# A long-convolution gate: the third stage's loop over rows instead of groups, and the distance between its two halves

## The chip, the cores and the metric

One core of a Trainium2 chip. The metric is the device time of one execution in microseconds (us), the median of several runs. The engines are TensorE (PE in the profile, its weight loads PEld), VectorE (DVE), ScalarE (ACT), GpSimd (POOL) and SyncE (SP, which only issues transfers here); DMA queues hang on SP and ACT.

## The reference

Two layers, all in float32, with B = 4 sequences of S = 12800 positions and D = 128 channels. The second uses the first's output y times x as its own input:

```python
def _attn_ref(x, v, pos_emb, w1, w2):
    h_filt = (np.maximum(pos_emb @ w1, 0.0) @ w2) * np.exp(-0.01 * pos)[:, None]
    u = x * v
    y = irfft(rfft(u, 2 * S) * rfft(h_filt, 2 * S))[:, :S, :]      # causal convolution along S
    return x * y

def _moe_ref(x, w_val, conv_w, w_out):          # x: what the first layer returned
    for k in range(5):
        gate_pre += conv_w[k] * xp[:, k:k + S, :]   # 5 taps along S, per channel
    gate = 1 / (1 + exp(-gate_pre))
    return (gate * (x @ w_val)) @ w_out
```

## The kernel before, in words

The convolution is done as Fourier transforms written as matrix products over S = 2 x 100 x 64 (J x N1 x N2). The first stage forms u = x·v, transforms it along N1 and stores the spectra in DRAM (`a_u`); the second multiplies them with the filter's spectrum and stores back-transformed blocks in DRAM (`c_y`). Both are untouched. The change lies in the **third stage** (from line 530), which does the last inverse transform along N1, multiplies by x, and runs the whole second layer.

Its unit is a **row**: one n2 of 64, that is 4 x 100 = 400 values in each of 128 channels (`ROW`). Four rows make a **group** (`R = 4`); 2 x 16 groups make the output (`NT = 32`, 128 rows). Two halves run at once, one ahead of the other.

*The y half* makes a row of x·y. `y_sum` (line 592): PE multiplies the blocks of `c_y` into PSUM `sd` (two buffers); two rows' sums stand together, at every second row. `y_copy` (601): ACT copies `sd` to `sd_sb`. Two rows later (`LAG = 2`) `y_trans` (606): PE transposes into `tp`, ACT copies a part to `dif`. `y_join` (615): DVE makes `yr` in two instructions (620, 621), POOL multiplies with x into `ext` (623). `ext` holds a block of 16 rows behind 4 rows of halo. The halo is filled by ACT (`fill_halo`, 576) once in four groups, after the last row of the block's first group is under way: one copy of 1600 wide (line 588), four narrower ones for the first block of a half (583 to 586), and one more copy of 1600 for the last (590). In each half of 16 groups the last group comes first, into a tile of its own, `tail`, because the first block's halo needs it.

*The gate half* reads 4 groups' rows from `ext`. `tap(t, 0)` (635): ACT starts group t's gate `gt` with the first tap, 1600 wide. `tap(t, 1)` to `tap(t, 4)` (638): DVE adds one tap to the whole group, one in each row's turn; tap k needs the group's first k rows. `sigmoid` (642): ACT, 1600 wide, after tap 4. In the next group's turn, row by row: `value` (647) PE into `v_ps`, `gated` (652) DVE into `gd`, one row later `project` (657) PE into `o_ps`, one more row later `finish` (665) ACT copies into `o_sb`, and after the fourth row ACT issues the group's store (668).

The order is written out by hand (`tc.manual_schedule()`): each engine executes its instructions in the order in which the loop records them, and waits only for semaphores. The loop (684) goes over groups, with four rows inside; the y half works on group `s = t + AHEAD3`, three groups, that is 12 rows, ahead of the group t that gets its taps. So the row r of a y group is always recorded together with the row r of a gate group: the sums stand with r = 0 and 2, the first tap of the next group and the sigmoid with r = 3, and the halo copy with r = 3 too, behind the sigmoid. Loads of the next blocks of `c_y` and of x (`load_rows`) are issued by SP, which waits there for free buffers.

Of the kernel before, what the change touches and what calls it, by code (L numbers as in the profile page):

```python
# [9 lines left out]
F32 = mybir.dt.float32  # L10
# [18 lines left out]
R = 4  # L29
# [92 lines left out]
def tile_longconv_gate(  # L122
# [407 lines left out]
    with tc.tile_pool(name="p3", bufs=1) as p3, tc.tile_pool(name="ps3", bufs=1, space=PSUM) as ps3:  # L530
# [17 lines left out]
        def load_rows(s):  # L548
            j, g = y_order[s]
            ct = []  # L550
            for c in range(2):
                t = block(s, c)
                ct.append(t)
                if s < FIRST:
                    continue
                n0 = c * N2 + g * R
                rows_ = c_y[j].rearrange("k p b d -> k p (b d)")
                for h in range(0, R, R // 2):
                    sync_s.dma_start(
                        out=t[:, h * B * D:(h + R // 2) * B * D],  # L560
                        in_=rows_[:, n0 + h:n0 + h + R // 2].rearrange("k p e -> k (p e)"))
            if s not in loads3:
                load_x(s)
            loads3[s] = ct, loads3[s]
# [27 lines left out]
        def y_sum(s, r):  # L592
            ct, _ = loads3[s]
            sd = ps3.tile([128, B * D], F32, name="sd", bufs=2)
            for c in range(2):
                nc.tensor.matmul(  # L596
                    out=sd[c * N2:(c + 1) * N2], lhsT=inv[:, c], rhs=ct[c][:, r * B * D:(r + 1) * B * D],
                    start=True, stop=True)
            sds[s, r] = sd

        def y_copy(s, r):
            t = p3.tile([128, B, D], F32, name="sd_sb", bufs=3)
            nc.scalar.copy(out=t.rearrange("p b d -> p (b d)"), in_=sds.pop((s, r)))  # L603
            sds[s, r] = t

        def y_trans(s, r):
            t = sds.pop((s, r))
            tp = ps3.tile([D, B, 128], F32, name="tp3", bufs=2)
            for b in range(B):
                nc.tensor.transpose(out=tp[:, b], in_=t[:, b], identity=ident)  # L610
            dif = p3.tile([D, B, NC1], F32, name="dif", bufs=3)
            nc.scalar.copy(out=dif, in_=tp[:, :, N2:N2 + NC1])
            tps[s, r] = tp, dif
# [17 lines left out]
        def tap(t, k):  # L631
            if k == 0:
                gt = p3.tile([D, R * ROW], F32, name="gt", bufs=2)
                gate_gt[t] = gt
                nc.scalar.activation(gt, rows(t, 0), AF.Copy, scale=cw[:, 0:1])  # L635
            else:
                gt = gate_gt[t]
                nc.vector.scalar_tensor_tensor(gt, rows(t, k), cw[:, k:k + 1], gt, op0=ALU.mult, op1=ALU.add)  # L638

        def sigmoid(t):  # L640
            sg = p3.tile([D, R * ROW], F32, name="sg", bufs=2)
            nc.scalar.activation(sg, gate_gt.pop(t), AF.Sigmoid)  # L642
            gate_sg[t] = sg

        def value(t, r):
            v_ps = ps3.tile([D, ROW], F32, name="v_ps", bufs=2)
            nc.tensor.matmul(out=v_ps, lhsT=wval, rhs=rows(t)[:, r * ROW:(r + 1) * ROW], start=True, stop=True)  # L647
            return v_ps

        def gated(t, r, v_ps):  # L650
            gd = p3.tile([D, ROW], F32, name="gd", bufs=2)
            nc.vector.tensor_tensor(gd, v_ps, gate_sg[t][:, r * ROW:(r + 1) * ROW], op=ALU.mult)  # L652
            return gd

        def project(gd):
            o_ps = ps3.tile([D, ROW], F32, name="o_ps", bufs=2)
            nc.tensor.matmul(out=o_ps, lhsT=wout, rhs=gd, start=True, stop=True)  # L657
            return o_ps

        def finish(t, r, o_ps):  # L660
            if r == 0:
                o_sb = p3.tile([D, R * ROW], F32, name="o_sb", bufs=2)
                outs3[t] = o_sb
            o_sb = outs3[t]
            nc.scalar.copy(out=o_sb[:, r * ROW:(r + 1) * ROW], in_=o_ps)  # L665
            if r == R - 1:
                j, g = groups[t]
                nc.scalar.dma_start(
                    out=out[j][:, g * R:(g + 1) * R].rearrange("d n b a -> d (n b a)"), in_=outs3.pop(t))

        AHEAD3, NT, LAG = 3, len(groups), 2
        y_run, gd_last, o_last = [], None, None
        with tc.manual_schedule():
            for s in range(2):
                load_x(s)
            load_rows(0)

            for _ in range(WARM):  # L680
                w_ps = ps3.tile([D, 2 * D], F32, name="o_ps", bufs=2)
                nc.tensor.matmul(
                    out=w_ps, lhsT=ident, rhs=dft.rearrange("p a k -> p (a k)"), start=True, stop=True)
            for t in range(-AHEAD3, NT + 2):
                s = t + AHEAD3
                if s + 1 < NT:
                    load_rows(s + 1)
                if 0 <= s < NT:
                    j, g = y_order[s]
                    if g == NG - 1:  # L690
                        tails[j] = p3.tile([D, R, B, N1], F32, name="tail", bufs=2)
                    elif g % EG == 0:
                        new_ext(j, g // EG)
                for r in range(R):
                    done = y_run.pop(0) if len(y_run) == LAG or s >= NT and y_run else None
                    if done:
                        y_trans(*done)
                    v_ps = value(t - 1, r) if 0 <= t - 1 < NT else None
                    if o_last is not None:
                        finish(*o_last)  # L700
                        o_last = None
                    if gd_last is not None:
                        o_last = gd_last[0], gd_last[1], project(gd_last[2])
                        gd_last = None
                    if s < NT and r % 2 == 0:
                        y_sum(s, r)
                        y_sum(s, r + 1)
                    if 0 <= t < NT:
                        tap(t, r + 1)
                    if r == R - 1 and 0 <= t + 1 < NT:  # L710
                        tap(t + 1, 0)
                    if v_ps is not None:
                        gd_last = t - 1, r, gated(t - 1, r, v_ps)
                    if done:
                        y_join(*done)
                    if s < NT:
                        y_copy(s, r)
                        y_run.append((s, r))
                    if r == R - 1 and 0 <= t < NT:
                        sigmoid(t)  # L720
                    if r == R - 1 and s < NT and g % EG == 0:
                        fill_halo(j, g // EG)


_INS = ["w1", "w2", "moe_w_val", "moe_conv_w", "moe_w_out"]
# [44 lines left out]
```

## Time and profile before

| what | value |
|---|---|
| median of three runs | 1163.94 us (1157.94, 1163.94, 1168.69) |
| profiled execution | 1167.67 us, its span 1165.5 us |
| third stage | from about 766 us to the end |
| busy in the span | PE 1046.1, DVE 969.3, POOL 775.2, ACT 615.7 us |
| busy, 900 to 1000 us | PE 97.0, DVE 96.3, POOL 88.8, ACT 72.5 of 100 us; DMA 0.94 |

The span goes from the first to the last instruction; the execution's own time is 2.2 us longer. In a row of the timeline the first number is the start in us, the second the duration; several instructions of one kind that follow each other are merged (x2). "idle before" in brackets is the time for which the engine had nothing to run, with what ended it. A duration includes the engine's pipeline, so that the next instruction can start up to 0.1 us before it ends; how often an engine can start an instruction is read from start to start.

### The profile page before, as it was taken

What the parts mean: (1) busy time and instruction counts of PE and PEld (TensorE: products, weight loads), DVE (VectorE), ACT (ScalarE), POOL (GpSimd) and SP (SyncE); (2) the same over time, 40 slices, a digit from 0 to 9 for tenths busy, and PEclk for the clock granted to TensorE, in tenths of its full rate; (3) what the DMA queues carried; (4) which work ended last, traced back from release to release, by engine and by line L of the source; (5) the groups of instructions that cost most, each with busy time, mean ns of one, the idle gap of its engine ahead of it and who ended that gap; (6) DMA issues with size and microseconds to landing.
All of it is one profiled execution on the core that took longest, in us unless ns stands there. A gap on an engine that the chain in (4) does not pass through costs nothing.

```text
span 1165.5 us, 17562 instructions
## 1 busy us (share of the span) xinstructions
PE 1046.1 (90%) x6208; PEld 492.1 (42%) x6208; DVE 969.3 (83%) x1150; ACT 615.7 (53%) x1000; POOL 775.2 (67%) x393
## 2 busy tenths in 40 slices
PE   4899887887764999999999999979999999999986
PEld 2455543443321444444444444434444444444432
DVE  5675445798944899999999999629999999999996
ACT  1366555665641344444444444346676767677763
POOL 3354332323313888889888889737889898898880
PEclk9999999998995899999999999988999999999999
DMA  9999999999987588988888998558999999999932
GB/s 364 350 417 403 361 352 345 353 341 350 344 268 286 209 311 300 317 300 302 303 312 287 362 339 321 178 176 218 283 288 285 264 292 278 278 289 284 284 119 113
DMA packets 92888, 344.60 MB, mean 296 GB/s; under 512 B 9774, under 2 KB 19418, under 8 KB 77610
## 3 DMA queue, kind: packets, MB, share of 16 engines
q1 hardware_dynamic: 58824, 263.74, 69.1%
q10 hardware_dynamic: 33978, 79.74, 17.8%
q8 instruction: 51, 0.84, 0.3%
q14 instruction: 35, 0.29, 0.1%
HBM read 212.37 MB, written 131.07 MB: 295 GB/s over the span
## 4 chain that ended last, share of the span: by engine, by line
PE 58%; DMA 28%; ACT 6%; DVE 4%; issue 2%; SPq 1%; ACTq 0%; DVEq 0%
PE c_ps L435 21%; DMA a_u<-st 19%; PE sd L596 9%; PE z_ps L419 9%; DMA ld<-in_xv_dram 6%; PE o_ps L657 6%; PE v_ps L647 5%; PE tp L610 5%; PE c_ps L404 2%; DVE gt L638 2%; PE fp L334 2%; ACT gt L635 1%; ACT o_sb L665 1%; DMA c_y<-c_sb 1%; ACT sg L642 1%
## 5 line engine op out<-in xcount | busy, mean ns | idle before, releaser
L623 POOL TENSOR_TENSOR ext<-yr,xr 128x400 f32<-128x400 f32 x120 | 301.6, 2515 | 44.0 <-DVE yr L621 41.9
L322 POOL TENSOR_TENSOR eo<-eo 128x512 f32<-128x512 f32 x62 | 116.8, 1904 | 212.0 <-DVE eo L321 212.0
L334 PE MATMUL fp<-eo,fold 64*128 64x512 f32 x768 | 194.4, 640 | 54.5 <-ACT st L336 40.1
L638 DVE SCALAR_TENSOR_TENSOR gt<-ext,cw,gt 128x1600 f32<-128x1600 f32 x128 | 241.5, 1887 | 0.8 <-ACT gt L635 0.8
L442 ACT COPY c_sb<-c_ps 128x1024 f32<-128x1024 f32 x100 | 101.3, 1013 | 204.6 <-PE c_ps L435 196.5
L336 ACT COPY st<-fp 128x1024 f32<-128x1024 f32 x128 | 124.2, 1015 | 133.2 <-DMA a_u<-st 81.5
L435 PE MATMUL c_ps<-va,ld 64*128 64x512 f32 (+1 forms) x800 | 166.6, 556 | 0.1
L425 DVE TENSOR_TENSOR va<-z_ps,h_sb 128x2048 f32<-128x2048 f32 x50 | 114.3, 2286 | 38.7 <-DMA ld<-a_u 30.4
L504 POOL TENSOR_TENSOR va<-va,vb 128x1024 f32<-128x1024 f32 x50 | 118.4, 2367 | 40.0 <-DVE vb L425 40.0
L419 PE MATMUL z_ps<-ld 64*64 64x512 f32 x800 | 122.4, 621 | 18.2 <-DMA ld<-a_u 16.3
L334 PEld LDWEIGHTS fp<-eo,fold 64*128 64x128 f32 x768 | 74.8, 197 | 135.8 <-issue 76.4
L596 PE MATMUL sd<-ag,inv 100*64 100x512 f32 x512 | 128.7, 620 | 1.6 <-ACT sd_sb L603 1.0
L657 PE MATMUL o_ps<-gd,wout 128*128 128x400 f32 x256 | 112.4, 521 | 19.7 <-DVE gd L652 10.9
L435 PEld LDWEIGHTS c_ps<-va,ld 64*128 64x128 f32 x800 | 74.2, 189 | 113.7 <-issue 110.2
L506 POOL TENSOR_TENSOR va<-va,vb 128x1024 f32<-128x1024 f32 x50 | 118.3, 2367 | 0.0
L603 ACT COPY sd_sb<-sd 128x512 f32<-128x512 f32 x128 | 76.1, 595 | 76.8 <-PE sd L596 54.1
L425 DVE TENSOR_TENSOR vb<-z_ps,h_sb 128x2048 f32<-128x2048 f32 x50 | 114.0, 2280 | 0.0
L647 PE MATMUL v_ps<-ext,wval 128*128 128x400 f32 x256 | 107.1, 500 | 0.0
L435 PE MATMUL c_ps<-vc,ld 64*128 64x512 f32 x400 | 94.2, 589 | 0.0
L610 PEld LDWEIGHTS tp<-ident,sd_sb 128*128 128x128 f32 x512 | 60.1, 144 | 78.9 <-PE sd L596 47.9
L505 POOL TENSOR_TENSOR vc<-vc,vd 128x768 f32<-128x768 f32 x50 | 91.2, 1824 | 2.2 <-issue 0.3
L610 PE MATMUL tp<-ident,sd_sb 128*128 128x128 f32 x512 | 81.9, 286 | 5.4 <-ACT sd_sb L603 3.8
(84 smaller groups left out, 1452.1 us busy)
## 6 DMA issues: line engine op xcount, KB each, us to landing
ld<-in_xv_dram SPq DMA_DIRECT2D x64, 1024.0 KB
c_y<-c_sb ACTq DMA_DIRECT2D x100, 512.0 KB
ld<-a_u SPq DMA_DIRECT2D x49, 1024.0 KB
a_u<-st SPq DMA_DIRECT2D x64, 768.0 KB
ag<-c_y SPq DMA_DIRECT2D x116, 384.0 KB
out_dram<-o_sb ACTq DMA_DIRECT2D x32, 800.0 KB
xr<-in_xt_dram SPq DMA_DIRECT2D x31, 800.0 KB
ld<-in_tab_w_dram SPq DMA_DIRECT2D x12, 768.0 KB
```

Source lines behind the costliest of these rows:

```text
L334: nc.tensor.matmul(out=fp[:, h], lhsT=fold[r, w], rhs=eo[r, o, :, l], start=i == 0, stop=i == len(terms) - 1)
L336: nc.scalar.copy(out=st[:, o].rearrange("k j (h b) d -> k h j (b d)", h=2), in_=fp)
L419: nc.tensor.matmul(out=zs[c][half[h]], lhsT=wk[half[c], 0, half[h]], rhs=a2[half[c], h, j], start=True, stop=True)
L425: nc.vector.tensor_tensor(out, z.rearrange("p (b d) -> p b d", d=D).unsqueeze(1).to_broadcast([128, n, B, D]), h_sb.unsqueeze(2).to_broadc ...
L435: nc.tensor.matmul(out=c_ps[:, h, 0:n], lhsT=wk[half[h], 1 + c], rhs=vt[half[h]].rearrange("p b d -> p (b d)"), start=(i == 0), stop=(i == ...
L504: nc.gpsimd.tensor_tensor(va[:, 0:2], va[:, 0:2], vb[:, 0:2], op=ALU.add)
L596: nc.tensor.matmul(out=sd[c * N2:(c + 1) * N2], lhsT=inv[:, c], rhs=ct[c][:, r * B * D:(r + 1) * B * D], start=True, stop=True)
L610: nc.tensor.transpose(out=tp[:, b], in_=t[:, b], identity=ident)
L623: nc.gpsimd.tensor_tensor(e[:, r0 + r], yr, xr, op=ALU.mult)
L638: nc.vector.scalar_tensor_tensor(gt, rows(t, k), cw[:, k:k + 1], gt, op0=ALU.mult, op1=ALU.add)
L647: nc.tensor.matmul(out=v_ps, lhsT=wval, rhs=rows(t)[:, r * ROW:(r + 1) * ROW], start=True, stop=True)
L657: nc.tensor.matmul(out=o_ps, lhsT=wout, rhs=gd, start=True, stop=True)
```

## The change

The loop goes over single rows. The y half's place (s, r) and the gate half's (t, rt) are both worked out from the row's number i, the second from i - 9: `AHEAD3` is 9 and counts rows. What is recorded within a row, and its order, is the same. Since 9 = 2·4 + 1, row r of a y group now stands together with row rt = r - 1 of a gate group: the first tap and the sigmoid (rt = 3) with r = 0, the halo copy (r = 3) with rt = 2, one row ahead of the next group's first tap and not behind the sigmoid. For the last group the sigmoid is four instructions of 400, and its output goes in three stores: rows 0 and 1, row 2, row 3.

```diff
         def sigmoid(t):
-            sg = p3.tile([D, R * ROW], F32, name="sg", bufs=2)
-            nc.scalar.activation(sg, gate_gt.pop(t), AF.Sigmoid)
+            sg, gt = p3.tile([D, R * ROW], F32, name="sg", bufs=2), gate_gt.pop(t)
+            step = ROW if t == NT - 1 else R * ROW
+            for c in range(0, R * ROW, step):
+                nc.scalar.activation(sg[:, c:c + step], gt[:, c:c + step], AF.Sigmoid)
             gate_sg[t] = sg
...
-            if r == R - 1:
-                j, g = groups[t]
+            j, g = groups[t]
+            r0 = {NT - 1: {1: 0, 2: 2, 3: 3}}.get(t, {R - 1: 0}).get(r)
+            if r0 is not None:
                 nc.scalar.dma_start(
-                    out=out[j][:, g * R:(g + 1) * R].rearrange("d n b a -> d (n b a)"), in_=outs3.pop(t))
+                    out=out[j][:, g * R + r0:g * R + r + 1].rearrange("d n b a -> d (n b a)"),
+                    in_=o_sb[:, r0 * ROW:(r + 1) * ROW])
...
-        AHEAD3, NT, LAG = 3, len(groups), 2
+        AHEAD3, NT, LAG = 9, len(groups), 2
...
-            for t in range(-AHEAD3, NT + 2):
-                s = t + AHEAD3
-                if s + 1 < NT:
-                    load_rows(s + 1)
-                if 0 <= s < NT:
+            for i in range(R * NT + AHEAD3 + R + 3):
+                (s, r), (t, rt) = divmod(i, R), divmod(i - AHEAD3, R)
+                if r == 0 and s < NT:
+                    if s + 1 < NT:
+                        load_rows(s + 1)
...
-                for r in range(R):
-                    done = y_run.pop(0) if len(y_run) == LAG or s >= NT and y_run else None
...
-                    if 0 <= t < NT:
-                        tap(t, r + 1)
-                    if r == R - 1 and 0 <= t + 1 < NT:
-                        tap(t + 1, 0)
...
+                if 0 <= t < NT:
+                    tap(t, rt + 1)
+                if rt == R - 1 and 0 <= t + 1 < NT:
+                    tap(t + 1, 0)
...
+                if s < NT:
+                    y_copy(s, r)
+                    y_run.append((s, r))
+                if rt == R - 1 and 0 <= t < NT:
+                    sigmoid(t)
+                if r == R - 1 and s < NT and g % EG == 0:
+                    fill_halo(j, g // EG)
```

Behind the diff line 642 becomes 644, 647 becomes 649, 652 becomes 654, 657 becomes 659, 665 becomes 667 and 668 becomes 671.

The order on ACT, at the start of the stage, before: from the last copy of the first halo (`tail`) to the first sigmoid's table.

```order
L586 COPY ext<-tail 128x16
L612 COPY dif<-tp_5574 128x204
L603 COPY sd_sb<-sd 128x512
L612 COPY dif<-tp_5593 128x204
L603 COPY sd_sb<-sd 128x512
L612 COPY dif<-tp_5606 128x204
L603 COPY sd_sb<-sd 128x512
L612 COPY dif<-tp_5625 128x204
L635 ACTIVATE gt<-ext,cw 128x1600
```

The same place in the changed kernel:

```order
L586 COPY ext<-tail 128x16
L612 COPY dif<-tp_5574 128x204
L635 ACTIVATE gt<-ext,cw 128x1600
L603 COPY sd_sb<-sd 128x512
L612 COPY dif<-tp_5595 128x204
```

The first tap (635) stood behind four `dif` copies after the halo; now it stands behind one.

The order on ACT where the second block of the first half gets its halo (line 588), before, with the numbers of the buffers:

```order
L612 COPY dif_5922<-tp3_5917 128x204
L665 COPY o_sb_5898<-o_ps_5900 128x400
L635 ACTIVATE gt_5930<-ext_5495,cw_73 128x1600
L603 COPY sd_sb_5938<-sd_5905 128x512
L642 ACTIVATE sg_5940<-gt_5817 128x1600
L588 COPY ext_5839<-ext_5495 128x1600
L612 COPY dif_5958<-tp3_5953 128x204
```

The same place in the changed kernel:

```order
L603 COPY sd_sb_5966<-sd_5934 128x512
L588 COPY ext_5865<-ext_5495 128x1600
L612 COPY dif_5984<-tp3_5979 128x204
L667 COPY o_sb_5955<-o_ps_5957 128x400
L635 ACTIVATE gt_5998<-ext_5865,cw_73 128x1600
L603 COPY sd_sb_6006<-sd_5991 128x512
L644 ACTIVATE sg_6008<-gt_5885 128x1600
L612 COPY dif_6015<-tp3_6010 128x204
```

Before, the three wide instructions (635, 642, 588) stand in one row, ahead of the next row's `dif`. Now the halo copy ends the row before, and the next row's `dif` and `o_sb` copies stand between it and the other two.

The end of ACT's order, before, from the last group's sigmoid on:

```order
L642 ACTIVATE sg<-gt 128x1600
L665 COPY o_sb<-o_ps 128x400 x2
L668 DMA out_dram<-o_sb 128x1600
L665 COPY o_sb<-o_ps 128x400 x4
L668 DMA out_dram<-o_sb 128x1600
```

And in the changed kernel:

```order
L644 ACTIVATE sg<-gt 128x400 x4
L667 COPY o_sb<-o_ps 128x400 x2
L671 DMA out_dram<-o_sb 128x1600
L667 COPY o_sb<-o_ps 128x400 x2
L671 DMA out_dram<-o_sb 128x800
L667 COPY o_sb<-o_ps 128x400
L671 DMA out_dram<-o_sb 128x400
L667 COPY o_sb<-o_ps 128x400
L671 DMA out_dram<-o_sb 128x400
```

The four parts of the sigmoid all stand ahead of the two copies of the group before; the last two rows get a store each.

More of the change, by code (lines that the diff above doesn't have):

```diff
@@ L693, in tile_longconv_gate @@
                         new_ext(j, g // EG)
-                for r in range(R):
-                    done = y_run.pop(0) if len(y_run) == LAG or s >= NT and y_run else None
[L696 to L707, printed above, removed]
-                    if 0 <= t < NT:
-                        tap(t, r + 1)
-                    if r == R - 1 and 0 <= t + 1 < NT:
-                        tap(t + 1, 0)
[L712 to L722, printed above, removed]
@@ new lines, in tile_longconv_gate @@
+                done = y_run.pop(0) if len(y_run) == LAG or s >= NT and y_run else None
+                if done:
+                    y_trans(*done)
+                v_ps = value(t - 1, rt) if 0 <= t - 1 < NT else None
+                if o_last is not None:
+                    finish(*o_last)
+                    o_last = None
+                if gd_last is not None:
+                    o_last = gd_last[0], gd_last[1], project(gd_last[2])
+                    gd_last = None
+                if s < NT and r % 2 == 0:
+                    y_sum(s, r)
+                    y_sum(s, r + 1)
@@ new lines, in tile_longconv_gate @@
+                if 0 <= t < NT:
+                    tap(t, rt + 1)
+                if rt == R - 1 and 0 <= t + 1 < NT:
+                    tap(t + 1, 0)
+                if v_ps is not None:
+                    gd_last = t - 1, rt, gated(t - 1, rt, v_ps)
+                if done:
+                    y_join(*done)
+                if s < NT:
[3 more added lines that the diff above has]
+                    sigmoid(t)
```

## The prediction

> **What bounds the kernel now.** I read busy time by stretch first, then the third stage's timeline, then the waits and the chain that ended last. The first two stages are untouched, so only the time from 766 us on counts. Two regular pairs of rows:
>
> ```profile
> 844.57:850.21 5.64, 5.64 (x26) 2.62 (x25) 5.64 (x10) 4.43 (x10) 5.23 (x3) 1.00 1.03 287
> 850.21:855.86 5.65, 5.65 (x26) 2.63 (x25) 5.65 (x10) 3.36 (x7) 5.23 (x3) 1.00 0.95 296
> ```
>
> The columns are the stretch, its length, busy PE, PEld, DVE, ACT and POOL, the granted clock, the DMA share and GB/s. In a regular pair PE and DVE are both full. The timeline of VectorE over one row shows which of the two sets the pace:
>
> ```profile
> 842.00 1.87 DVE L638 SCALAR_TENSOR_TENSOR gt<-ext,cw,gt 128x1600 f32<-128x1600 f32 x1
> 843.79 0.56 DVE L652 TENSOR_TENSOR gd<-v_ps,sg 128x400 f32<-128x400 f32 x1
> 844.27 0.36 DVE L620 TENSOR_TENSOR yr<-tp,dif 128x204 f32<-128x204 f32 x1
> 844.55 0.35 DVE L621 TENSOR_TENSOR yr<-tp,dif 128x196 f32<-128x196 f32 x1
> 844.82 1.87 DVE L638 SCALAR_TENSOR_TENSOR gt<-ext,cw,gt 128x1600 f32<-128x1600 f32 x1
> ```
>
> From start to start: tap 1.79, gated product 0.48, the two `yr` 0.28 and 0.27; the row is their sum, 2.82 us, with no gap. VectorE is the bound; PE fills the same time but waits for `gd` in it. So the question for every part is where VectorE, from its first tap to its last, stands still. In the steady part that is one place:
>
> ```profile
> DVE yr L620 <- ACT dif L612: 10.1, 7, 2.4
> ...
> 819.32 1.53 ACT gt L635
> ...
> 959.47 1.53 ACT gt L635
> ...
> 1006.03 1.53 ACT gt L635
> ...
> 1123.61 1.53 ACT gt L635
> ```
>
> Seven waits of 10.1 us in all, the only ones of VectorE between 801 and 1131 us. The first and the last of the chain rows are 26 groups apart: 304.29 us, where 104 rows of 2.8215 (two rows took 5.643) make 293.4. The excess, **10.9 us**, is these seven waits and what little follows them; they are the seven halo copies after the first.
>
> **Why a halo stops VectorE, and what the new phase does to it.** ScalarE's row with a first tap (before: r = 3) and, for one with a halo, the end of that row:
>
> ```profile
> 842.25 0.33 ACT L612 COPY dif<-tp 128x204 f32<-128x204 f32 x1 [0.82 <-PE tp L610]
> 842.48 0.50 ACT L665 COPY o_sb<-o_ps 128x400 f32<-128x400 f32 x1
> 842.86 1.64 ACT L635 ACTIVATE gt<-ext,cw 128x1600 f32<-128x1600 f32 x1
> 844.40 0.58 ACT L603 COPY sd_sb<-sd 128x512 f32<-128x512 f32 x1
> 844.86 1.55 ACT L642 ACTIVATE sg<-gt 128x1600 f32<-128x1600 f32 x1
> 846.30 0.34 ACT L612 COPY dif<-tp 128x204 f32<-128x204 f32 x1
> ...
> 868.88 1.53 ACT L588 COPY ext<-ext 128x1600 f32<-128x1600 f32 x1
> 870.30 0.35 ACT L612 COPY dif<-tp 128x204 f32<-128x204 f32 x1
> ...
> 870.75 0.37 DVE L620 TENSOR_TENSOR yr<-tp,dif 128x204 f32<-128x204 f32 x1 [0.99 <-ACT dif L612]
> ...
> 1105.14 0.37 DVE L620 TENSOR_TENSOR yr<-tp,dif 128x204 f32<-128x204 f32 x1 [2.42 <-ACT dif L612]
> ```
>
> From start to start: `dif` 0.23, `o_sb` 0.38, tap 1.54, `sd_sb` 0.46, sigmoid 1.44, halo 1.42. Without a halo the next `dif` starts at 846.30 and is ready at 846.64, and its `yr` would run at 847.10: 0.46 spare. A halo adds 1.42, so VectorE waits 0.96 (0.99 in the row); two copies add 2.84, so 2.38 (2.42). The account closes, so I use it for the new order.
>
> Zero is now the start of VectorE's tap in the heavy row, which is r = 0. Before, it stands at 842.00, and PE's `tp` lets the heavy row's `dif` start at 0.25; two sums stand ahead of that `tp`. In the new order no sums stand ahead of r = 0's `tp`, but they do ahead of the row before, so that row (zero at -2.82) has `dif` from -2.57, `o_sb` -2.34 and `sd_sb` -1.96 to -1.50. Without a halo the heavy row then runs with nothing late. With one:
>
> halo -1.50, `dif` -0.08, `o_sb` 0.15, tap 0.53, `sd_sb` 2.07, sigmoid 2.53 to 4.08, next `dif` 3.97 to 4.31.
>
> VectorE needs the heavy row's `dif` at 2.27, the sigmoid at 2.82 + 1.79 = 4.61 and the next `dif` at 5.09. All are there; the tightest has 0.53 spare. The halo is hidden in ScalarE's idle time ahead of the heavy row. Two copies push by another 1.42: the sigmoid ends at 5.50, VectorE waits **0.89**, twice. The four narrow copies of the second half's first block take 0.3 more than one (959.47 to 1006.03, 46.56 for 16 rows with this halo; with a single copy 45.14 + 1.1): within the spare. So of 10.9 us 1.8 stay: **-9.1**. Bounds: -10.9 if the double copies are hidden too, 0 if the wait only changes its name. I take the middle of the account, since it gave both old waits to 0.04.
>
> **The shorter lead itself.** Taps wait for products of POOL. A row's product ends a row after its join (POOL, 5.23 busy in the pair's 5.64, runs one to a row); tap k follows the join of its last row by 3 rows now, by 6 before. Two rows of cover are left; the price if they went is one shift of the pipeline, not one in each row. The start and the drain change:
>
> ```profile
> 780.02 0.34 ACT L612 COPY dif<-tp 128x204 f32<-128x204 f32 x1
> 780.24 0.60 ACT L603 COPY sd_sb<-sd 128x512 f32<-128x512 f32 x1
> ...
> 784.63 1.63 ACT L635 ACTIVATE gt<-ext,cw 128x1600 f32<-128x1600 f32 x1
> ...
> 786.30 2.32 DVE L638 SCALAR_TENSOR_TENSOR gt<-ext,cw,gt 128x1600 f32<-128x1600 f32 x1 [0.47 <-ACT gt L635]
> ...
> 1140.51 1.87 DVE L638 SCALAR_TENSOR_TENSOR gt<-ext,cw,gt 128x1600 f32<-128x1600 f32 x1
> 1142.30 0.56 DVE L652 TENSOR_TENSOR gd<-v_ps,sg 128x400 f32<-128x400 f32 x1
> 1142.79 1.87 DVE L638 SCALAR_TENSOR_TENSOR gt<-ext,cw,gt 128x1600 f32<-128x1600 f32 x1
> ```
>
> The first tap now stands right behind the `dif` of 780.02, so it starts at 780.24, where `sd_sb` did, and not at 784.63: 4.4 earlier, and VectorE's first tap with it. Three rows of the y half that ran ahead of the taps now run beside them: each costs VectorE two `yr`, 0.55, together 1.6 (a drain row is 2.28, a full one 2.82). **-2.8**. Bounds: -4.4 if the `yr` find gaps, 0 if what `sd_sb` loses behind the early tap holds up the next rows.
>
> **The end.** The last sigmoid, what waits for it, and the last store:
>
> ```profile
> 1153.80 1.54 ACT L642 ACTIVATE sg<-gt 128x1600 f32<-128x1600 f32 x1 [2.52 <-DVE gt L638]
> 1155.24 0.87 ACT L665 COPY o_sb<-o_ps 128x400 f32<-128x400 f32 x2
> 1155.36 1.22 DVE L652 TENSOR_TENSOR gd<-v_ps,sg 128x400 f32<-128x400 f32 x2 [1.12 <-ACT sg L642]
> ...
> 1156.08 0.91 PE L657 MATMUL o_ps<-gd,wout 128*128 128x400 f32 x2
> ...
> 1161.23 0.34 ACTq L668 DMA_DIRECT2D out_dram<-o_sb  x1
> ...
> 1162.00:1163.00 1.00, 0.00 (x0) 0.00 (x0) 0.00 (x0) 0.00 (x0) 0.00 (x0) 1.00 0.97 410
> 1163.50:1164.00 0.50, 0.00 (x0) 0.00 (x0) 0.00 (x0) 0.00 (x0) 0.00 (x0) 1.00 1.03 410
> ```
>
> The parts give `gd` its first row about 1 us sooner. But project 1156.08 also needs the `o_ps` buffer that the first of the two copies frees, and these copies stand behind all four parts, which at the 0.38 of a 400-wide copy take 1.52, not 1.44. It gains what the copy lets through: about **-0.1** (bounds +0.3 and -1). The store: issued 1161.23, data from 1162 to 1164, the span's end 1165.5. A quarter of the bytes takes 0.5 of the 2.0: **-1.5**, if the two stores ahead, issued about 2.3 and 1 us earlier, are through; were the three in series, each with the 0.8 ahead and the 1.5 behind its data, it would be 1158.9 + 3.3 + 2.8 + 2.8 = 1167.8, +2.3. I take -1.5, since data ran at 410 GB/s as soon as it came. The Trainium skill has a rule against the split: "DMA: Bandwidth & Descriptors", "Rules for kernel authors", tells to join many small transfers, since under 64 KB they are mostly overhead; its "Anatomy of one DMA" gives a fixed part of about 2.0 us for each. The trace's own fixed part is 0.8 + 1.5 = 2.3, for one store; whether three overlap no row here shows, and a row's store has 200 KB. By the page's 2.0, an estimate with the fixed parts in series, the end would be 1158.9 + 3.0 + 2.5 + 2.5 = 1166.9, +1.4 and not -1.5.
>
> **The sum.** -9.1 - 2.8 - 0.1 - 1.5 = -13.5. On the profiled execution: 1167.67 - 13.5 = 1154.2. It stands 3.7 above the median of 1163.94; from the median, **1150.5 us**, 1.2% faster.
>
> **The rivals.** *A. The halo's time stays.* The wait goes to another place, or to the transfers: the DMA shares above, 1.03 and 0.95 in two regular pairs, are near full, and four groups with the wait in them may be what the transfers can do. Against it: no wait of PE for a load of `c_y` stands in the steady part, and three groups of four already run without the halo's pause. Then -4.4: 1159.5.
>
> *B. The clock.* At the stage's start PE runs at half clock for 6.8 us:
>
> ```profile
> 785.90:789.30 3.40, 1.67 (x8) 0.63 (x9) 3.00 (x4) 2.32 (x6) 1.08 (x2) 0.93 1.01 310
> 789.30:792.70 3.40, 3.38 (x10) 1.47 (x12) 3.40 (x4) 0.65 (x3) 3.40 (x2) 0.50 1.03 242
> 792.70:796.10 3.40, 3.40 (x14) 1.95 (x10) 3.40 (x5) 1.28 (x3) 3.40 (x2) 0.56 0.38 72
> ```
>
> A stretch with PE busy 1.67 of 3.40 precedes it, and it costs nothing, since VectorE stays full: these rows have no `value` and `project` yet. The earlier tap holds PE up earlier. If the slow stretch falls on full rows, where PE's work fills the row at full clock, half its 6.8 us is lost: +3.4, 1153.9. The Trainium skill, "TensorE: Matmul & The Clock Gate", Part 1, says that an idle window of some 3.4 us halves the clock; here a half-idle one came before it.
>
> *C. Slower.* The sigmoid now stands between the copies of the two sums, (s, 0) and (s, 1). PE's next sums (r = 2, 0.52 behind that row's tap, so at 6.16) need both buffers. By the account with a halo, (s, 1) is copied from 4.58 to 5.2, one us ahead. If ScalarE is over 1 us later than that, PE waits in each group. Such waits in the stage now:
>
> ```profile
> PEld sd L596 <- ACT sd_sb L603: 3.8, 5, 1.9
> ```
>
> That is 0.76 each; 31 groups make 23.6, which swallows the halo's gain: 1163.9 - 4.4 + 23.6 = 1183.1. Against it: without a halo the sigmoid starts as tap 4 ends, at 1.9, 0.6 sooner, so three groups in four have over 1.5 us to spare.
>
> **How the numbers follow.** Forecast 0.66, A 0.18, B 0.10, C 0.06. A measurement of this kernel can tell about 1% from no change; 1% is 11.6 us, at 1152.3. Two thirds of the forecast's cases and a third of B's lie below that: 0.47, with a little for fills and ends that do better, 0.49. C is slower: 0.06. The rest, 0.45, is within 1%. The range: the bounds add to -10.9 - 4.4 - 1.0 - 1.5 = -17.8 (1146.1), and A lies at 1159.5; with a us more on either side for the spread of the median, 1145 to 1160.5. C is left out.
>
> **What would show it.** Right: VectorE's waits for `dif` gone but for two of about 0.9, now for the sigmoid; the heavy rows' chain rows 45.15 apart; the first tap 14.3 behind the first `tp`, not 18.7; the last store's issue to the end under 3 us. Wrong: waits of PE for `sd_sb` or for loads in each group, or a half clock behind the first `project`.

## The result and the profile after

| what | before | after |
|---|---|---|
| median of four runs each | 1164.89 us (1157.94 to 1168.69) | **1148.27 us** (1147.54 to 1149.53) |
| ratio, with its 95% interval | | **0.9859** (0.9825 to 0.9893) |
| profiled execution | 1167.67 us | 1147.54 us |
| first `tp` of the third stage, on PE | 765.97 us | 760.08 us |
| from there to the end of the execution's span | 399.5 us | 385.7 us |

Faster by 1.4%; 1150.5 was forecast. Ratios, here and below, leave out executions in which the chip ran in a slower state. The profiled executions differ by 20.1 us, but only **13.8** of them lie in the third stage, the only part that the change touches. 5.9 us went before its first `tp`, in stages whose code is the same (0.4 lie outside the two spans): in 14 traces of this study that `tp` starts anywhere between 755.3 and 766.0 us, with no regard to the kernel. So everything below is measured from the stage's first `tp` or first `yr` (1.5 us later), and not from the total.

The steady part of the stage first: busy PE, PEld, DVE, ACT and POOL between 800 and 1100 us, then the granted clock, the DMA share and GB/s. Before:

```profile
800.00:1100.00 300.00, 292.57 (x1232) 134.31 (x1232) 291.96 (x414) 210.93 (x372) 268.12 (x103) 1.00 0.94 279
```

After:

```profile
800.00:1100.00 300.00, 298.36 (x1270) 138.17 (x1269) 298.43 (x425) 218.13 (x381) 271.76 (x106) 1.00 0.97 289
```

VectorE stood still for 8.0 us of these 300 before and stands still for 1.6 now; the number of its instructions in brackets shows that it got 11 more of them through. The waits of VectorE of the changed kernel between 796 and 1112 us are one line, where before there were seven waits for `dif`, of 10.1 us:

```profile
DVE gt L638 <- ACT gt L635: 1.6, 2, 0.8
```

Two waits are left, as forecast, but for ScalarE's first tap and not for its sigmoid. They belong to the two double halo copies. Here is the first, on ACT and DVE (start, duration, engine and line):

```profile
907.27 1.55 ACT L588 COPY ext<-ext 128x1600 f32<-128x1600 f32 x1
...
908.70 1.54 ACT L590 COPY ext<-tail 128x1600 f32<-128x1600 f32 x1
...
910.12 0.35 ACT L612 COPY dif<-tp 128x204 f32<-128x204 f32 x1
910.34 0.52 ACT L667 COPY o_sb<-o_ps 128x400 f32<-128x400 f32 x1
910.53 0.57 DVE L654 TENSOR_TENSOR gd<-v_ps,sg 128x400 f32<-128x400 f32 x1
910.73 1.67 ACT L635 ACTIVATE gt<-ext,cw 128x1600 f32<-128x1600 f32 x1
...
912.43 2.01 DVE L638 SCALAR_TENSOR_TENSOR gt<-ext,cw,gt 128x1600 f32<-128x1600 f32 x1 [0.79 <-ACT gt L635]
```

The two copies, the next `dif` and `o_sb` come in the order that the prediction's list gave, and the first tap is done at 912.40, just ahead of the VectorE tap that needs it. A single halo is hidden altogether. These two first taps of ScalarE have one between them:

```profile
852.11 1.64 ACT L635 ACTIVATE gt<-ext,cw 128x1600 f32<-128x1600 f32 x1
...
897.28 1.64 ACT L635 ACTIVATE gt<-ext,cw 128x1600 f32<-128x1600 f32 x1
```

45.17 us for four groups, and the forecast was 45.15.

The stage's start, in the profiled execution:

```profile
760.08 1.11 PE L610 MATMUL tp<-ident,sd_sb 128*128 128x128 f32 x4 [3.81 <-ACT sd_sb L603]
...
775.27 0.34 ACT L612 COPY dif<-tp 128x204 f32<-128x204 f32 x1
775.49 1.65 ACT L635 ACTIVATE gt<-ext,cw 128x1600 f32<-128x1600 f32 x1
...
777.17 1.97 DVE L638 SCALAR_TENSOR_TENSOR gt<-ext,cw,gt 128x1600 f32<-128x1600 f32 x1 [0.82 <-ACT gt L635]
```

The first tap stands right behind the one `dif`, 15.4 us after the first `tp`, where 14.3 was forecast and 18.7 was the old distance. In a second trace of the same kernel (below, as a repeat) it is 14.1. The 1.3 us between the two is the granted clock. Here are the second pair of sums and the two microseconds from 6 us behind the first `tp` on (the clock is the third number from the end), first in this trace:

```profile
766.63 2.75 PE L596 MATMUL sd<-ag,inv 100*64 100x512 f32 x8
...
766.08:768.08 2.00, 2.00 (x7) 0.76 (x8) 1.27 (x4) 0.95 (x3) 1.11 (x2) 0.50 1.04 244
```

And in the repeat:

```profile
771.45 1.94 PE L596 MATMUL sd<-ag,inv 100*64 100x512 f32 x8
...
771.41:773.41 2.00, 2.00 (x11) 0.57 (x10) 1.28 (x4) 1.35 (x4) 1.21 (x2) 1.00 1.04 256
```

The stage starts at half clock in every trace, and the first transposes and sums are slow by it. Here the half clock lasted until 8.2 us behind the first `tp`, in the repeat until 5.5, so that one more pair of sums fell into it (2.75 us and not 1.94), and part of the transposes ahead of it (1.97 and not 1.45).

And the end, from the last sigmoid on:

```profile
1135.53 1.81 ACT L644 ACTIVATE sg<-gt 128x400 f32<-128x400 f32 x4 [2.52 <-DVE gt L638]
1137.24 0.86 ACT L667 COPY o_sb<-o_ps 128x400 f32<-128x400 f32 x2
...
1143.01 0.34 ACTq L671 DMA_DIRECT2D out_dram<-o_sb  x1
```

The span ends at 1145.8, 2.8 us behind the issue of the last store and not 4.3.

### The profile page after: what moved, and what is told of

Same layout as the page of the kernel before. It is cut to its first block, busy times and chain, and to the rows that moved or that the text cites. A ratio compares the mean times of both kernels' runs of the same rounds, so it can differ in the third digit from the quotient of the medians.

```text
span 1145.8 us, 17528 instructions
## 1 busy us (share of the span) xinstructions
PE 1041.9 (91%) x6208; PEld 490.5 (43%) x6208; DVE 969.1 (85%) x1150; ACT 615.9 (54%) x1003; POOL 781.2 (68%) x393
## 4 chain that ended last, share of the span: by engine, by line
PE 66%; DMA 24%; DVE 5%; ACT 3%; issue 1%; SPq 0%; ACTq 0%; DVEq 0%
PE c_ps L435 22%; DMA a_u<-st 13%; PE sd L596 10%; PE z_ps L419 9%; DMA ld<-in_xv_dram 8%; PE o_ps L659 7%; PE v_ps L649 6%; PE tp L610 5%; PE fp L334 3%; PE c_ps L404 2%; DMA ld<-in_pos_dram 2%; DVE gt L638 1%; DVE fk L284 1%; ACT st L336 1%; PE gp L292 1%
## 5 line engine op out<-in xcount | busy, mean ns | idle before, releaser
L322 POOL TENSOR_TENSOR eo<-eo 128x512 f32<-128x512 f32 x62 | 120.0, 1954 | 204.6 <-DVE eo L321 204.6
L659 PE MATMUL o_ps<-gd,wout 128*128 128x400 f32 x256 | 111.5, 517 | 10.7 <-DVE gd L654 8.7
```

Of the source, the lines that this page charges most:

```text
L322: eng.tensor_tensor(eo[:, s, :, 0], eo[:, s, :, 0], eo[:, s, :, 1], op=ALU.subtract)
```

## The experiments

Every kernel has the third stage's start and end in its trace, so beside the device times this table gives, for each, stretches in us: from the first `yr` to VectorE's first tap; from there to the tap that follows the first gated product (the first group's inside); on to the last tap; from the last tap to the end of the span; and the sum, which is called the stage below. The expectations of ctl12, halo_r0_12, lead13 and lead9 count the stage from the first `tp`, 1.5 us earlier.

| kernel | to first tap | first group | to last tap | end | sum |
|---|---|---|---|---|---|
| before | 18.82 | 15.10 | 350.49 | 13.61 | 398.02 |
| after | 15.58 | 13.00 | 343.45 | 12.18 | 384.21 |
| ctl12: lead 12 | 18.92 | 15.10 | 350.50 | 13.62 | 398.14 |
| halo_r0_12: lead 12, halo moved | 17.95 | 15.10 | 341.38 | 13.63 | 388.06 |
| lead13 | 19.69 | 13.89 | 341.25 | 13.64 | 388.47 |
| lead11 | 16.58 | 13.08 | 347.30 | 13.63 | 390.59 |
| lead11_store2 | 16.59 | 13.07 | 342.52 | 13.63 | 385.81 |
| lead9 | 15.63 | 13.01 | 343.44 | 13.63 | 385.71 |
| lead9_store0 | 14.16 | 13.00 | 377.15 | 13.69 | 418.00 |
| lead8 | 13.38 | 14.68 | 352.56 | 13.67 | 394.29 |
| end12: lead 12, new end | 19.12 | 15.09 | 350.52 | 12.12 | 396.85 |
| lead9_store: lead 9, stores split | 14.65 | 13.45 | 343.45 | 12.08 | 383.63 |
| after, again | 14.25 | 13.00 | 343.43 | 12.10 | 382.78 |
| best | 14.37 | 13.00 | 341.42 | 11.73 | 380.52 |

The first column differs by up to 1.5 us between executions with the same order. That is the clock again: of the six with 9 rows, after and lead9 had the half clock until 8.2 and 8.5 us behind the first `tp` and show 15.6, the other four until 5.2 to 6.2 us, with 14.2 to 14.7. The other columns repeat to 0.1 where nothing but that start differs (lead9_store's first group excepted).

**The loop alone** (ctl12): the loop over rows with the old distance and the old end.

```diff
-        AHEAD3, NT, LAG = 9, len(groups), 2
+        AHEAD3, NT, LAG = 12, len(groups), 2
...
-            step = ROW if t == NT - 1 else R * ROW
+            step = R * ROW
...
-            r0 = {NT - 1: {1: 0, 2: 2, 3: 3}}.get(t, {R - 1: 0}).get(r)
+            r0 = {R - 1: 0}.get(r)
```

> The row loop with the y half 12 rows ahead and the end as before: every engine's order is that of the kernel before, only line numbers differ. Theory: no change, ratio 1.000 +- 0.003, third stage (first transpose to the span's end) 399.5 us. Rival (part of the change's 16.6 us lies in the first two stages, because the program was built anew): 0.997, with the first transpose about 3 us or more earlier than 766 us.

1163.78 us beside 1163.15, ratio 1.0011 (0.9987 to 1.0035), and every stretch of the stage within 0.1 us of before. Its waits of VectorE:

```profile
DVE yr L620 <- ACT dif L612: 10.1, 7, 2.4
DVE gd L654 <- ACT sg L644: 0.7, 1, 0.7
DVE gt L638 <- ACT gt L635: 0.4, 1, 0.4
```

So writing the loop over rows does nothing; all the rest comes from the distance and the end.

**The halo copy alone** (halo_r0_12): still 12 rows ahead, but each halo copy is recorded one row later, so that it no longer stands behind the first tap and the sigmoid in the same row.

```diff
-                if r == R - 1 and s < NT and g % EG == 0:
-                    fill_halo(j, g // EG)
+                sh = (i - R) // R
+                if r == 0 and 0 <= sh < NT and y_order[sh][1] % EG == 0:
+                    fill_halo(y_order[sh][0], y_order[sh][1] // EG)
```

> Lead of 12 rows and end as before; only the halo copy stands one row later, at the end of row r = 0 and not behind the sigmoid of r = 3. Theory (ScalarE's three wide copies in one row stop VectorE): single halos cost nothing, the two double ones about 0.7 us each; third stage 399.5 - 9.5 = 390 us, ratio 0.992. Rival (the gain is the shorter lead's own): no gain, ratio 1.000. Rival (transfers set the pace of the steady part): no gain either, and waits of PE for loads of c_y appear.

1155.81 us, ratio 0.9938 (0.9915 to 0.9961). The stretch to the last tap falls by 9.1 us and the waits for `dif` from seven to two:

```profile
DVE yr L620 <- ACT dif L612: 1.4, 2, 0.7
```

One copy's place in ScalarE's order is worth what the prediction gave to the halos, with the lead and all else unchanged. VectorE has no wait that it did not have before. ScalarE's waits that the profile puts down to loads of `c_y` rise from 5.9 to 16.6 us, but they don't reach VectorE. From the first `tp` the stage is 389.6 us; 390 was expected.

**The phase without a shorter lead** (lead13): 13 rows have the same phase as 9 (r of the y half stands with rt = r - 1), but are longer than 12.

```diff
-        AHEAD3, NT, LAG = 9, len(groups), 2
+        AHEAD3, NT, LAG = 13, len(groups), 2
```

with the old end.

> Lead of 13 rows: the same phase of the two halves as with 9 (13 = 3*4 + 1), but a lead that is longer than before. End as before. Theory: the halo's part of the gain stays (-8.7 us), one more row of lead costs 0.9 us (1.45 of a row ahead of the taps, less 0.55 for two yr): third stage 391.7 us, ratio 0.993. Rival (the lead itself makes the gain, about 4 us a row): slower than before, 403.5 us, ratio 1.003.

Six runs from 1138.93 to 1165.99 us, ratio 0.986 (0.979 to 0.993): too wide for much. The trace says more: 388.5 where ctl12, the same loop, has 398.1. So 9.7 of the gain come with a **longer** lead, and the phase carries them. From the first `tp` it is 390.0, 1.7 better than expected.

**The change without its end** (lead9).

```diff
-        AHEAD3, NT, LAG = 13, len(groups), 2
+        AHEAD3, NT, LAG = 9, len(groups), 2
```

against lead13, with the old end.

> The change without its end: lead of 9 rows, the last group's sigmoid and store whole. Theory: the end is worth 1.4 us, so third stage 385.7 + 1.4 = 387.1 us, 15.2 us behind 9 would be the kernel before with the first stages' difference; ratio 0.9875 where the whole change has 0.9859. From the last tap's start to the span's end 13.6 us as before. Rival (the end is worth nothing, its three receipts come one after another): 385.7 us and the same ratio as the whole change.

1151.62 us, ratio 0.9907 (0.9874 to 0.9941); stage 385.7, or 387.2 from the first `tp`, where 387.1 was expected. Against lead13, four rows at equal phase are 2.8 us. But this trace is one of the two with the longer half clock at its start, and lead13 is not; the repeat of the change with the old end's 1.5 us put back would have 384.3, and four rows then are 4.2 us. So a row of lead is worth **0.7 to 1.0 us**, the three rows of the change 2.1 to 3.1, and the rest of the gain over ctl12, 10.3 to 10.7, goes with the phase (with what happens inside the first group, below).

**One row less** (lead8): the phase in which r of both halves is the same, as before, with the halo copy taken to the end of r = 2, ahead of the heavy row.

```diff
-        AHEAD3, NT, LAG = 9, len(groups), 2
+        AHEAD3, NT, LAG = 8, len(groups), 2
...
-                if r == R - 1 and s < NT and g % EG == 0:
+                if r == 2 and s < NT and g % EG == 0:
```

> Lead of 8 rows, so that row r of a y group stands with row r of a gate group again (8 = 2*4), as with 12; the halo copy is recorded at the end of row r = 2, the last place ahead of the tap that reads it. End as before. Theory (the phase decides, not the lead): the halo copy must wait for POOL's product of the row before it, 2.82 us behind that row's tap, the first tap then ends at 3.67 where VectorE's next group wants it at 2.82: a wait of about 0.85 us at each of seven halos, and up to 0.1 us in rows where taps now meet POOL's products; third stage from the first yr to the span's end 385.7 (lead 9) - 0.7 + 6 = 391 us or more, slower than lead 9 although the lead is shorter. Rival (every row of lead less gains): 385 us.

1161.07 us in one execution, stage 394.3: 8.6 over lead9, although it starts its taps earlier. The waits of VectorE, and the one of ScalarE that causes them:

```profile
DVE gt L638 <- ACT gt L635: 6.3, 6, 1.4
DVE yr L620 <- ACT dif L612: 1.7, 2, 0.8
DVE gt L638 <- POOL ext L623: 1.2, 1, 1.2
```

```profile
ACT ext L588 <- POOL ext L623: 3.1, 6, 0.5
```

The halo copies, one row earlier in the y group, now wait for POOL to finish the last row that they copy, and the first tap stands behind them; nine waits of VectorE, 9.2 us where lead9 has 1.6, make up most of the 8.6. Here the shorter lead does not pay, because its phase leaves the halo no free place.

**Two rows more** (lead11): another phase, r with rt = r + 1.

```diff
-        AHEAD3, NT, LAG = 9, len(groups), 2
+        AHEAD3, NT, LAG = 11, len(groups), 2
```

with the old end.

> Lead of 11 rows: the first tap and the sigmoid stand with r = 2, the halo copy with r = 3, one row behind them and not in their row. End as before. Theory: any phase but r = rt keeps the halo from VectorE; between lead 13 (388.5 us from the first yr to the span's end) and lead 9 (385.7), so 387.1 us, with waits for dif gone in the steady part. Rival (only the phase of 9 and 13 does it): about 397 us, with seven waits for dif of 10 us in all.

1153.0 us in one execution; stage 390.6, and 387.1 was expected: a miss. VectorE waits for 6.1 us between 796 and 1112 us where lead9 has 1.6. The trace shows ScalarE standing still, in waits that the profile puts down to whatever came last; none of these three is in lead9:

```profile
ACT sd_sb L603 <- DMA ag<-c_y: 40.8, 11, 5.7
ACT sd_sb L603 <- PE tp L610: 28.9, 10, 3.4
ACT sd_sb L603 <- PE v_ps L649: 17.0, 5, 4.0
```

One of them with SyncE's issues beside it (SPq and ACTq rows are issues of transfers):

```profile
821.75 5.50 SPq L118 DMA_DIRECT2D ag<-c_y  x8
...
823.83 0.50 ACT L667 COPY o_sb<-o_ps 128x400 f32<-128x400 f32 x1
...
828.47 0.34 ACTq L671 DMA_DIRECT2D out_dram<-o_sb  x1
...
828.85 0.58 ACT L603 COPY sd_sb<-sd 128x512 f32<-128x512 f32 x1 [4.53 <-DMA ag<-c_y]
```

`o_sb` is complete at 824.33, and the group's store that is to follow is issued at 828.47, after SyncE's eight loads of the next block. ScalarE executes in order, so `sd_sb` stood behind it for 4.5 us. The 32 stores of lead11 are issued 2.9 us in the median, and at most 5.3, behind the end of the `o_sb` copy ahead of them; in lead9 it is 0.03 us, and never more than 0.04. With 11 rows the store is recorded with r = 0, where SyncE issues the next group's loads; with 9 it is recorded with r = 2. That was a theory after the fact, so the last two kernels move nothing but the store.

**The store out of the loads' way, and into it** (lead11_store2, lead9_store0): each group's store is recorded two rows later, and the last one at its old place.

```diff
+                if late and late[0][0] <= i:
+                    _, dst, src = late.pop(0)
+                    nc.scalar.dma_start(out=dst.rearrange("d n b a -> d (n b a)"), in_=src)
...
             if r0 is not None:
-                nc.scalar.dma_start(
-                    out=out[j][:, g * R + r0:g * R + r + 1].rearrange("d n b a -> d (n b a)"),
-                    in_=o_sb[:, r0 * ROW:(r + 1) * ROW])
+                late.append((i + (2 if t < NT - 1 else 0), out[j][:, g * R:(g + 1) * R], o_sb))
```

> The lead of 11 rows, the end as before, and each group's store recorded two rows later, with r = 2 and not with r = 0 of the y half; the last group's store stays at its end. Theory: at a lead of 11 the stage was 3.5 us longer than its place on the line between 13 and 9 rows, because ScalarE stood behind the store's issue while SyncE issued the next group's eight loads. Two rows later these loads are out: ScalarE's waits put down to the loads of c_y (40.8 us, 11 times) go, and from the first yr to the end 390.6 becomes 387.1 (386.5 to 388). Rival: the time goes with the row in which the heavy work stands (first tap and sigmoid with r = 2, behind the sums of r = 0) and not with the store: 390.6, and the waits stay under another name.

> The lead of 9 rows, the end as before, and each group's store recorded two rows later, with r = 0 and not with r = 2 of the y half, just ahead of the first tap of the heavy row. Theory: r = 0 is where SyncE issues the next group's loads, so the store's issue holds ScalarE up there, by up to 4 us in a group and in the row with the least spare: from the first yr to the end 385.7 becomes at least 395 (up to 425), with waits of VectorE for ScalarE's first tap. Rival: the place of the store does not matter, 385.7 within 1 us; then what cost time at 11 rows was the place of the heavy row.

Both go with the theory. lead11_store2: 1150.86 us, stage 385.8 (387.1 was the middle of the expectation, 386.5 its lower end), 4.8 less than lead11, and ScalarE's waits put down to loads are gone. It is that short although a slower clock cost this execution 2.0 us early on (under the rivals, below). Between 800 and 1100 us VectorE has not one gap:

```profile
800.00:1100.00 300.00, 300.00 (x1280) 140.92 (x1279) 300.00 (x428) 223.87 (x387) 276.26 (x106) 1.00 0.96 287
```

lead9_store0: 1176.56 us, stage 418.0, **32.3 us longer** than lead9 for the same instructions with the store two rows later; at least 395 was expected. ScalarE waits in nearly every group ahead of the first tap, and VectorE behind it:

```profile
ACT gt L635 <- DMA xr<-in_xt_dram: 50.4, 23, 3.3
```

```profile
823.61 6.09 SPq L118 DMA_DIRECT2D ag<-c_y  x8
...
827.94 0.34 ACTq L705 DMA_DIRECT2D out_dram<-o_sb  x1
...
828.33 1.63 ACT L635 ACTIVATE gt<-ext,cw 128x1600 f32<-128x1600 f32 x1 [2.33 <-DMA xr<-in_xt_dram]
...
829.99 1.88 DVE L638 SCALAR_TENSOR_TENSOR gt<-ext,cw,gt 128x1600 f32<-128x1600 f32 x1 [1.07 <-ACT gt L635]
```

25 such waits of VectorE make 29.5 us. The store was issued here while the last of SyncE's eight loads was still to come (it starts at 829.46), so it does not simply queue behind all of them; what the two queues share, no trace here shows.

**The new end alone** (end12): lead 12, with the sigmoid and the stores of the last group in parts.

```diff
-        AHEAD3, NT, LAG = 9, len(groups), 2
+        AHEAD3, NT, LAG = 12, len(groups), 2
```

> The end alone: lead 12 as before, the last group's sigmoid in four and its store in three. Theory: from the last tap's start to the span's end 12.2 us and not 13.6, nothing else moves; from the first yr to the span's end 398.1 - 1.4 = 396.7 us. Rival (the three stores' fixed parts add up): 13.6 us or more.

1159.78 us in one execution; the last stretch 12.12 where ctl12 has 13.62: -1.50.

**The split stores without the split sigmoid** (lead9_store).

```diff
-            step = ROW if t == NT - 1 else R * ROW
+            step = R * ROW
```

> The whole change but with the last sigmoid in one piece. Theory: the split of the sigmoid is worth nothing (project waits for the o_ps copies behind it): from the last tap's start to the span's end 12.2 us, within 0.15 us of the whole change's 12.18. Rival (gd a us earlier is worth a us): 13.2 us.

1152.58 us in one execution; the last stretch 12.08, and 12.18 and 12.10 in the two traces with the sigmoid in parts. Its sigmoid and copies:

```profile
1140.62 1.54 ACT L644 ACTIVATE sg<-gt 128x1600 f32<-128x1600 f32 x1 [2.52 <-DVE gt L638]
1142.07 0.87 ACT L667 COPY o_sb<-o_ps 128x400 f32<-128x400 f32 x2
```

From the sigmoid's start to the copies 1.45 us, in four parts (rows of after, above) 1.71. What the first `gd` gains, the copies behind the four parts give back: the sigmoid's split is worth nothing.

**A repeat of the change** (after_again), measured beside the next kernel.

> The changed kernel once more, beside the next one and the same runs of the kernel before. Theory: third stage 384.2 us from the first yr to the span's end, 13.9 less than before, so a ratio of 0.988; what was measured beyond that, 16.6 us, is the spread of the first two stages, whose end lay between 760.1 and 766.0 us in the six traces so far. Rival (the whole 16.6 us is the change's): 0.986 again, and the first transpose earlier than in the kernels with the old lead.

1150.81 us over 6 runs beside 1163.29 over 11, ratio 0.9901 (0.9869 to 0.9934); stage 382.8, where 384.2 was expected (the clock at the start, above). The first measurement was 0.9859: together faster by 1.0 to 1.4%.

**What the readings suggest** (best): the second of a double halo, the copy from `tail`, three rows later, where ScalarE has time; and at the very end the copy of the group before ahead of the last sigmoid.

```diff
-            if q == NG // EG - 1:
-                nc.scalar.copy(out=e[:, EG * R:], in_=tails[j])
...
+                if r == 2 and 0 <= s < NT and g == NG - EG + 1:
+                    nc.scalar.copy(out=exts[j, NG // EG - 1][:, EG * R:], in_=tails[j])
...
+                if rt == R - 1 and t == NT - 1:
+                    finish(*o_last)
+                    o_last = None
                 if rt == R - 1 and 0 <= t < NT:
                     sigmoid(t)
```

> The changed kernel, with the copy of the tail into ext (line 590) three rows later, apart from the halo copy, and with the o_ps copy that the last sigmoid kept waiting put ahead of it. Theory: the two waits of 0.8 us of VectorE for the first tap go (-1.6 us), and the end gains 0.3 us: third stage 382.3 us from the first yr to the span's end, ratio to the kernel before 0.986 where the changed kernel has 0.988. Rival (the copy finds no idle time of ScalarE in its new row either): 384 us.

1145.99 us, ratio to before 0.9865 (0.9832 to 0.9897); its median is 0.996 of that of the repeat beside it, a difference less than the spread of either. The stage is 380.5, 2.3 below the repeat: the last waits are gone,

```profile
800.00:1100.00 300.00, 300.00 (x1276) 139.30 (x1274) 300.00 (x428) 219.52 (x385) 276.47 (x108) 1.00 0.97 291
```

and the end is 0.4 shorter. VectorE's work is now the whole of the steady part; a further gain there must take work from it.

## Why the prediction held

| term | forecast | measured | from |
|---|---|---|---|
| halos | -9.1 | -8.6 | stretch to the last tap, -7.0, less the 1.6 of three more full rows |
| start | -4.4 | -5.3 | to the first tap -3.2 (repeat: -4.6), first group -2.1 |
| three rows' `yr` beside taps | +1.6 | +1.6 | 3 x 0.55; lead9 against lead13, to the last tap: +2.2 for four rows |
| sigmoid in parts | -0.1 | 0 | lead9_store |
| store in parts | -1.5 | -1.4 to -1.6 | after, end12, lead9_store |
| sum | -13.5 | -13.8 | -15.2 in the second trace |

*The halos.* The account of ScalarE's row, started at VectorE's heavy tap, gave both the hidden single copy (45.17 us in four groups) and two waits of 0.89 for the doubled one (0.8 each measured). Their place was wrong: the list of 2.53 to 4.08 for the sigmoid was compared with what VectorE needs of the sigmoid, but not the row of the first tap, 0.53 to 2.07, with the next group's tap 1, which VectorE starts at 2.82. Pushed by 1.42 it starts at 1.95 and, 1.64 long, ends at 3.59, so VectorE waits 0.77 (0.79 measured), and the sigmoid is then just in time (done at 914.31, its gated product starts at 914.37). The earlier wait swallowed the one foreseen. Whether the phase or the lead does it is shown: moving only the copy is worth 9.1, and a lead of 13 rows gives 9.7.

*The start.* The first tap does stand behind the one `dif`; to VectorE's first tap that gave 3.2 in the first pair of traces, with the longer half clock in the changed kernel alone, and 4.6 in the second; the 4.4 was right. What the prediction left out is the first group's inside, 15.10 to 13.00. The second group's first tap on VectorE and the first gated product, before:

```profile
797.03 2.65 DVE L638 SCALAR_TENSOR_TENSOR gt<-ext,cw,gt 128x1600 f32<-128x1600 f32 x1 [0.37 <-ACT gt L635]
...
800.36 0.57 DVE L652 TENSOR_TENSOR gd<-v_ps,sg 128x400 f32<-128x400 f32 x1 [0.67 <-ACT sg L642]
```

and after:

```profile
787.11 2.11 DVE L638 SCALAR_TENSOR_TENSOR gt<-ext,cw,gt 128x1600 f32<-128x1600 f32 x1
789.14 0.56 DVE L654 TENSOR_TENSOR gd<-v_ps,sg 128x400 f32<-128x400 f32 x1
```

Two waits, of 0.37 and 0.67, are gone and taps are shorter, as of 2.65 there is 2.11. What took them away stays open. lead13, in the new phase, still has 13.89, and the clock may have a part in it: in before and lead13 7 us at half clock lie over the first group, in after 3.5, in the repeat none, and lead9_store, with the order of after, has 13.45 with 7 us of it. The two waits also stand right behind before's slow stretch, so that the prediction's word that it cost nothing is not shown. With the paid-back 1.6 the start was worth -3.7, in the repeat -5.1, and not -2.8.

*The end.* Three overlapping stores cost no fixed part one after another: 1.5 was gained, where a serial sum had +2.3. The Trainium skill, "DMA: Bandwidth & Descriptors", "Rules for kernel authors", tells to join small transfers; the prediction's estimate by that page's 2.0 us, in series, was +1.4, and the page gives the figure for transfers issued by GpSimd, not by ScalarE as here. The measurement decides otherwise: the parts overlap, and only the last one's stands at the end.

*The rivals.* A, the halo's time turning up elsewhere, is refuted by halo_r0_12 and by best: at a DMA share of 0.97 VectorE is busy for 300.00 of 300 us, so the transfers were not what held the stage. B, the clock: besides the longer half clock at the very start, which cost 1.3 us, it was granted at half speed here, too, from 778.6 to 782.0, behind a stretch with PE half busy,

```profile
774.30:777.75 3.45, 1.54 (x11) 0.51 (x6) 1.22 (x3) 3.45 (x8) 1.87 (x2) 1.00 0.00 0
777.75:781.16 3.41, 3.41 (x12) 1.02 (x12) 3.41 (x4) 1.49 (x4) 1.39 (x1) 0.62 0.01 2
```

but there VectorE is full, 3.41 of 3.41. B's own case, a half clock on full rows, came in another run, lead11_store2, and it cost a wait of 1.98 us, where B had put 3.4:

```profile
799.52 0.57 DVE L654 TENSOR_TENSOR gd<-v_ps,sg 128x400 f32<-128x400 f32 x1 [1.98 <-PE v_ps L649]
...
795.10:798.50 3.40, 3.40 (x12) 1.18 (x9) 2.44 (x4) 0.59 (x1) 3.13 (x2) 0.50 1.02 241
```

In the changed kernel one trace has this later slow stretch and the repeat has none, so that B stayed away is in part luck. The Trainium skill, "TensorE: Matmul & The Clock Gate", Part 1, asks for an idle window ahead of a halved clock; in the 3.4 us ahead of the drop PE was busy for 2.0 us in before and 1.5 in after. C, PE's sums behind the `sd_sb` copies: no wait of a sum for `sd_sb` is left between 796 and 1112 us; before there was one, of 0.9. But something like C exists, one row away: a ScalarE held up in each group does cost 32 us, when a store is what holds it (lead9_store0).

*The size.* From 1163.94 the sum gave 1150.5; the two medians are 1148.27 and 1150.81. That they come so close is in part luck: the medians carry the first two stages' spread, the profiled pair, 20.1 apart, would have flattered the change by six microseconds of them, and within the stage the first group's 2.1, which the prediction did not have, was partly offset by the 1.3 of the longer half clock.

## What to carry over

Where two halves of a pipeline share an in-order engine, the distance between them in rows sets which of its long instructions fall into one row; that phase can be worth more than the distance itself (over 10 us to 2 or 3 here), and adding up that engine's row from the neighbour's first need tells in advance whether a copy is hidden. Compare each item of such a row with its first reader, not only the last one. When a transfer is issued from a computing engine, look at what the other queue issues in the same rows: the place of a store cost 32 us at one distance and 5 at another.

## What the chip showed unasked

A store issued by ScalarE came out up to 5.3 us late while SyncE issued its eight loads of the next block (issue at 1059.70 for data complete at 1054.42 in lead11), and in lead9_store0 the same eight loads took 5.8 to 6.9 us to issue behind 800 us, 6.1 in the median, where lead9, without the meeting, has 4.4 to 6.1 and 4.8 in the median. In lead11 the loads were not slower, 4.6 in the median. Which resource they share stays open. And the first `tp` of the stage moved by 10.7 us over 14 executions in which the code ahead of it was the same: it was not followed up. The stage itself, in one order, moved by no more than 1.5 us in these traces.
